# Gated mix of attention and MLP (decode step): the query matrix first in the queue, in eight transfers of 16 partitions

## The chip, the core and the metric

The kernel runs on one core of one Trainium2 chip. The metric is the device time of one launch in microseconds; the time before is the median of three runs. Times inside an execution are counted from the start of the profile's span.

## The reference

For a batch of 8 rows `x` of width 576 (one token each), two branches are computed and mixed by a gate:

```python
g = sigmoid((x * gate_w).sum(-1))
q = x @ wq                            # 576 x 4096: 32 heads of 128
k, v = last 2048 keys of 8192         # 16 kv heads, two query heads share one
a = softmax(q k^T * 128**-0.5) v @ wo # 4096 x 576
b = gelu(layernorm(x) @ w1 + b1) @ w2 + b2   # 576 -> 4608 -> 576
out = g * a + (1 - g) * b
```

All inputs are bf16. What has to be read is mostly the cache: 8 x 16 heads x 2048 keys x 128, for K and for V, 134 MB; the four weight matrices are another 20 MB.

## The kernel before

**Placing and order.** All SBUF data lie in one tensor, `arena`, cut by hand into named regions. Every piece of work is entered in a plan (`_Plan.add`, `_Plan.dma`) with its dependencies; the plan gives each engine its order, and `emit` writes the instructions with semaphore waits. `after=` fixes an order without a wait.

**The load stream.** All large loads go through SyncE's DMA queue (SP), one behind the other, in this order: the small rest of `wq` (rows 512 to 575, 512 KB, L412), the big part of `wq` (rows 0 to 511, 4096 KB, L413), the big part of `w1` (4608 KB, L415), its rest (576 KB, L416), then 32 items of 4096 KB (K and V for 16 units of work, L618), then `w2` (L866) and `wo` (L836). The items go round four slots of 4 MB in the region `RAW`; `wq` lies in slot 0 to begin with and `w1` in slot 3, so that the first items in these slots wait until TensorE has used the matrices (`slot_free = [[o_qp], [], [], [o_hp], ...]`). The first two items, K0 and K1, have free slots and wait for nothing.

**The big part of `wq`.** Partition p of the 128 gets four rows of the matrix, 4p to 4p+3, which are 32 KB in one piece. One transfer carries all 128 partitions (L413). Every other large transfer, too, writes all 128 partitions; K, V and `wq` in rows of 32 KB, `w1` in rows of 36 KB.

**The small inputs.** `x` (8 x 576, partitions 0 to 7, L407), `gate_w` (one row on partition 0, L408), `b1` (four rows on partitions 0 to 3, L409) and `b2` (one row, L856) are issued from ScalarE (ACT), in its own queue, as its first four instructions.

**What the first loads feed.** `x` goes to VectorE (a copy, L421; sums for the layernorm, L433 on) and is transposed by TensorE (L452); `gate_w` is spread over 8 partitions by TensorE (L427) and gives the gate. TensorE's order at the start is: transposes of `x`, the gate's product, the transposes of the normalised `x`, the gate's spreading (L465, L466), then the query product `o_qp` (L501, which waits for both parts of `wq`), then the first product of the MLP, `o_hp` (which waits for `w1` and `b1`), then the bias of the second one (which waits for `b2`). After that the units follow: VectorE transposes K (L718, waits for the K item), TensorE computes the scores (L732), VectorE takes the maximum (L645), ScalarE the exponentials (L649), TensorE multiplies with V (L755 and L188).

**The end.** The products with `w2` and `wo` (L579) follow the last unit; two halves of the output are copied by VectorE and ScalarE (L901, L902) and written by one DMA from SP and one from ACT (L904).

Of the kernel before, what the change touches and what calls it, by code (L numbers as in the profile page):

```python
# [38 lines left out]
class _Plan:  # L39
# [10 lines left out]
    def add(self, eng, fn, deps=(), name=None, cost=0.1, after=(), prio=0):  # L50
        op = _Op(eng, fn, deps, name, cost, after=after, prio=prio)
        op.idx = len(self.all)
        self.all.append(op)
        return op

    def dma(self, eng, fn, semkey, nbytes, deps=(), name=None, after=(), prio=0):
        op = _Op(eng, fn, deps, name, self.DMA_ISSUE, after=after, is_dma=True, dma_sem=semkey, nbytes=nbytes, prio=prio)
        op.idx = len(self.all)
        self.all.append(op)
        return op  # L60
# [106 lines left out]
def _pst(t):  # L167
    return t.ap().ap[0][0]
# [26 lines left out]
def build_kernel(nc, A_x, A_k_cache, A_v_cache, A_wq, A_wo, B_x, B_w1, B_b1, B_w2, B_b2, gate_w, out):  # L195
    B, Sq, D = A_x.shape
    _, Hkv, Sk, Dh = A_k_cache.shape
    Hq = A_wq.shape[1] // Dh
    F = B_w1.shape[1]
# [12 lines left out]
    FC, FT = 4, 36  # L212
# [9 lines left out]
    x2 = A_x.rearrange("b s d -> (b s) d")  # L222
    out2 = out.rearrange("b s d -> (b s) d")

    with ExitStack() as es:
# [70 lines left out]
        arena = es.enter_context(nc.sbuf_tensor("arena", [128, (aoff[0] + 1) // 2], BF))  # L296
        AST = _pst(arena)
        arena_f = arena.bitcast(F32)

        def aoffs(name):  # L300
            return R[name][0] // 2
# [4 lines left out]
        def view(name, parts=128):  # L306
            o, n, dt = R[name]
            a = arena[0:parts, o // 2: o // 2 + (n * (2 if dt == BF else 4)) // 2]
            if dt == F32:
                a = a.bitcast(F32)  # L310
            return a
# [18 lines left out]
        b2_sb = view("b2", 1)  # L330
# [3 lines left out]
        ob = view("ob", 1)  # L334
# [10 lines left out]
        RAW = view("RAW")  # L345
        x_sb, gw_sb, y_bf = view("x_sb", 8), view("gw_sb", 1), view("y_bf", 8)
# [3 lines left out]
        b1c = view("b1c", FC)  # L350
# [4 lines left out]
        wq_m = RAW[:, 0:4 * 4096].rearrange("p (t c) -> p t c", t=4)  # L355
        W1O = (ND - 1) * DE
        WQR = W1O + 4 * F + F // 2
        wq_r = RAW[:, WQR:WQR + 2048]
        w1_m = RAW[:, W1O:W1O + 4 * F].rearrange("p (t c) -> p t c", t=4)
# [20 lines left out]
        add, dma = P.add, P.dma  # L380
# [23 lines left out]
        o_on8 = add("pool", lambda e: e.memset(ones8, 1.0), name="ones8", cost=0.15)  # L404


        d_x = dma("act", lambda e: e.dma_start(x_sb, x2), "x", 8 * D * 2, name="d_x")  # L407
        d_gw = dma("act", lambda e: e.dma_start(gw_sb, gate_w.partition_broadcast(1)), "g", D * 2, name="d_gw", after=[d_x])  # L408
        d_b1 = dma("act", lambda e: e.dma_start(b1c, B_b1.rearrange("(c f) -> c f", c=FC)), "b", F * 2, name="d_b1", after=[d_gw])  # L409
        dx = [d_x]  # L410
        db = [d_b1]
        d_wqr = dma("sp", lambda e: e.dma_start(wq_r, A_wq[512:576, :].rearrange("k (s c) -> (k s) c", s=2)), "wq", 64 * 8192, name="d_wqr")  # L412
        d_wqm = dma("sp", lambda e: e.dma_start(wq_m.rearrange("p t c -> p (t c)"), A_wq[0:512, :].rearrange("(p t) c -> p (t c)", t=4)), "wq", 512 * 8192, name="d_wqm", after=[d_wqr])  # L413
        dwq = [d_wqm, d_wqr]
        d_w1m = dma("sp", lambda e: e.dma_start(w1_m.rearrange("p t c -> p (t c)"), B_w1[0:512, :].rearrange("(p t) c -> p (t c)", t=4)), "w1", 512 * F * 2, name="d_w1m", after=[d_wqm])  # L415
        d_w1r = dma("sp", lambda e: e.dma_start(w1_r, B_w1[512:576, :].rearrange("k (s c) -> (k s) c", s=2)), "w1", 64 * F * 2, name="d_w1r", after=[d_w1m])  # L416
        dw1 = [d_w1m, d_w1r]

# [52 lines left out]
        o_obh = add("act", lambda e: e.activation(out=ob[:, 0:8], in_=ps[0:1, BK_X, 412:420], func=ACTF.Copy), deps=[o_gp, o_homg], name="ob_hi", cost=0.12)  # L471
        o_ob32 = add("act", lambda e: e.activation(out=ot32, in_=ob[:, 0:8], func=ACTF.Copy), deps=[o_obh], name="ob_32", cost=0.12)
        o_obl = add("dve", lambda e: e.tensor_tensor(out=ob[:, 8:16], in0=ps[0:1, BK_X, 412:420], in1=ot32, op=ALU.subtract), deps=[o_ob32], name="ob_lo", cost=0.12)
# [77 lines left out]
        o_hp = add("pe", h_fn, deps=dw1 + db + [o_yT, o_xT, o_gcol, o_homg, o_sel4, o_obl], name="h_pe", cost=5.0)  # L551
# [292 lines left out]
        o_m2, o_bias = [], []  # L844
# [8 lines left out]
            o_m2.append(add("pe", fn, deps=[exp_done[NU - 1], o_mrow, o_mcol], name=name, cost=0.21 * n, after=after))  # L853

        def bias(i):
            d = dma("act", lambda e: e.dma_start(b2_sb, B_b2.partition_broadcast(1)), "b2", D * 2, name="d_b2", after=[d_b1])  # L856
            o_bias.append(AccGroup("m2_b", [(ob[:, 0:8], b2_sb), (ob[:, 8:16], b2_sb)], [d, o_obl, o_obh], cost=0.6, after=[o_hp]).op)

        def m2_chunk(ci):
            s = take_slot()  # L860
# [14 lines left out]

        query(0)
        bias(0)
        for kind, i in stream:
            {"K": k_item, "V": v_item, "W": wo_chunk, "M": m2_chunk, "B": bias}[kind](i)
# [34 lines left out]
def bass_gated_mix__sliding_block_cached__mixer_channel_mlp__decode_kernel(  # L914
    nc: bass.Bass,
    A_x: bass.AP,
    A_k_cache: bass.AP,
    A_v_cache: bass.AP,
    A_wq: bass.AP,
    A_wo: bass.AP,  # L920
    B_x: bass.AP,
    B_w1: bass.AP,
    B_b1: bass.AP,
    B_w2: bass.AP,
    B_b2: bass.AP,
    gate_w: bass.AP,
    out: bass.AP,
):
    build_kernel(nc, A_x, A_k_cache, A_v_cache, A_wq, A_wo, B_x, B_w1, B_b1, B_w2, B_b2, gate_w, out)
# [28 lines left out]
```

## Time and profile before

| | us |
|---|---|
| median of 3 runs | 365.01 (364.51 to 365.36) |
| profiled execution, its own time | 364.83 |
| its span, first to last instruction | 363.3 |
| outside the span | 1.5 |
| VectorE busy | 235.6 |
| TensorE busy (modelled ends) | 299.2 |
| DMA: moved, mean rate over the span | 154.45 MB, 425 GB/s |

The profile's DMA rows give the mean busy share of the core's 16 DMA engines and what they moved. `SPq` and `ACTq` mark the issue of a DMA by that engine's sequencer. In the list of DMA issues the last number is the time from issue to landing. In the table of stages each row has the stretch, its length, the busy time and number of instructions of each engine, the clock granted to TensorE, the DMA share (packets are booked where they start, so that it can pass 1) and the rate.

### The profile page before, as it was taken

The page shows a single profiled execution, that of the slowest core. Times are in us where ns is not written, and L with a number is a line of the kernel's source. Part 1 is how long each engine was busy: PE and PEld are TensorE (multiplying, and loading weights), DVE is VectorE, ACT ScalarE, POOL GpSimd, SP SyncE. Part 2 cuts the span into 40 slices and gives each one's busy share as a digit, 9 for nine tenths or more (in the row PEclk, how much of TensorE's full clock was granted, in tenths as well). Part 3 has the DMA queues.
Part 4 walks back from the last instruction along what each step waited for, and adds up shares of the span by engine and source line. Part 5 has one row for each costly group of instructions (what it writes and reads, how often), then busy time and mean ns, then how long its engine had stood idle before and what let it go on. Part 6 is the DMA issues. An engine that isn't in the chain of part 4 may idle for free.

```text
span 363.3 us, 4819 instructions
## 1 busy us (share of the span) xinstructions
PE 299.2 (82%) x1954; PEld 125.4 (35%) x1423; DVE 235.6 (65%) x166; ACT 168.6 (46%) x130; POOL 22.9 (6%) x52
## 2 busy tenths in 40 slices
PE   1456367999999979998897979898989698999875
PEld 0100000434252615342433417150606152436742
DVE  5522979576776694929385758565675949294720
ACT  1112106656657463664637363838374654655000
POOL 9230030000010000000100000000000000003000
PEclk9976586999999998999999989999999999999999
DMA  8999999999999999999999999999999999999995
GB/s 349 433 429 413 447 419 451 415 451 415 447 415 447 419 448 417 444 422 451 415 455 411 453 411 458 408 458 406 458 411 455 415 449 415 447 419 443 413 430 245
DMA packets 6118, 154.45 MB, mean 425 GB/s; under 512 B 702, under 2 KB 856, under 8 KB 1244
## 3 DMA queue, kind: packets, MB, share of 16 engines
q1 hardware_dynamic: 6064, 154.28, 98.6%
q8 instruction: 8, 0.13, 0.1%
q10 hardware_dynamic: 44, 0.03, 0.1%
q14 instruction: 2, 0.02, 0.0%
HBM read 154.29 MB, written 0.01 MB: 425 GB/s over the span
## 4 chain that ended last, share of the span: by engine, by line
DMA 62%; DVE 24%; PE 12%; SPq 1%; issue 0%
DMA arena<-in_A_k_cache_dram 56%; DVE arena L718 21%; DMA arena<-in_B_w_dram 6%; PE ps L175 5%; DVE arena L668 2%; PE ps L188 2%; PE ps L755 2%; PE ps L732 2%; DVE arena L645 1%; PE ps L579 0%; SPq L415 0%; SPq L416 0%; DVE arena L901 0%; SPq L413 0%; SPq L412 0%
## 5 line engine op out<-in xcount | busy, mean ns | idle before, releaser
L718 DVE STREAM_TRANSPOSE arena<-arena 128x4096 f32<-128x4096 f32 (+1 forms) x34 | 141.7, 4175 | 21.4 <-DMA arena<-in_A_k_cache_dram 21.2
L674 ACT ACTIVATE arena<-arena 32x2048 bf16<-32x2048 bf16 x60 | 114.5, 1908 | 71.2 <-DVE arena L668 42.6
L175 PE MATMUL ps<-arena 128*128 128x512 bf16 (+3 forms) x531 | 137.2, 406 | 0.0
L188 PE MATMUL ps<-arena 128*128 x840 | 109.5, 277 | 7.0 <-issue 0.7
L188 PEld LDWEIGHTS ps<-arena 128*128 x840 | 81.3, 97 | 34.0 <-issue 19.0
L732 PE MATMUL ps<-arena 128*128 128x512 bf16 x128 | 51.2, 400 | 27.4 <-DVE arena L718 25.4
L645 DVE TENSOR_REDUCE arena<-ps 128x1 f32<-128x2048 f32 x16 | 36.7, 2292 | 55.4 <-PE ps L175 55.4
L732 PEld LDWEIGHTS ps<-arena 128*128 128x128 bf16 x128 | 12.6, 98 | 133.1 <-issue 77.0
L649 ACT ACTIVATE arena<-ps,arena 128x2048 bf16<-128x2048 f32 x16 | 40.6, 2540 | 0.5
L646 ACT ACTIVATE arena<-arena 128x1 f32<-128x1 f32 x16 | 3.2, 203 | 64.2 <-DVE arena L645 64.2
L755 PE MATMUL ps<-arena 128*128 128x256 bf16 x184 | 25.3, 273 | 1.2 <-DVE arena L663 1.1
L755 PEld LDWEIGHTS ps<-arena 128*128 128x128 bf16 x184 | 16.9, 99 | 19.3 <-issue 15.0
L668 DVE STREAM_TRANSPOSE arena<-arena 128x1024 f32<-128x1024 f32 x15 | 18.1, 1206 | 2.9 <-ACT arena L649 2.9
L579 PE MATMUL ps<-arena 128*8 128x288 bf16 (+1 forms) x140 | 9.9, 290 | 4.2 <-DMA arena<-in_A_wo_dram 3.2
L739 POOL MEMSET arena<- 128x4096 f32 x1 | 3.5, 3511 | 148.2 <-PE ps L175 148.2
L685 PE MATMUL ps<-arena 128*128 128x512 bf16 x16 | 6.5, 406 | 6.5 <-ACT arena L649 5.2
L629 POOL COPY arena<-arena 32x64 bf16<-32x64 bf16 x16 | 3.7, 229 | 128.2 <-PE ps L175 122.7
L452 PE MATMUL ps<-arena 8*128 8x8 bf16 x8 | 0.6, 171 | 12.8 <-DVE arena L433 7.0
L902 ACT ACTIVATE arena<-ps 8x288 bf16<-8x288 f32 x1 | 0.4, 401 | 19.7 <-PE ps L579 19.7
L579 PEld LDWEIGHTS ps<-arena 128*8 128x8 bf16 (+1 forms) x140 | 5.8, 86 | 10.3 <-issue 3.4
L557 DVE TENSOR_TENSOR arena<-arena 128x1152 f32<-128x1152 f32 x1 | 1.4, 1359 | 11.6 <-ACT arena L555 11.6
L901 DVE CAST arena<-ps 8x288 bf16<-8x288 f32 x1 | 0.4, 446 | 12.3 <-PE ps L579 12.3
(106 smaller groups left out, 101.5 us busy)
## 6 DMA issues: line engine op xcount, KB each, us to landing
arena<-in_A_k_cache_dram SPq DMA_DIRECT2D x16, 4096.0 KB, 28.7
arena<-in_A_v_cache_dram SPq DMA_DIRECT2D x16, 4096.0 KB, 25.5
arena<-in_B_w_dram SPq DMA_DIRECT2D x1, 4608.0 KB, 23.4
arena<-in_A_wo_dram SPq DMA_DIRECT2D x2, 2304.0 KB, 24.0
arena<-in_A_wq_dram SPq DMA_DIRECT2D x1, 4096.0 KB, 13.0
arena<-in_B_w_dram SPq DMA_DIRECT2D x1, 3456.0 KB, 24.4
arena<-in_B_w_dram SPq DMA_DIRECT2D x1, 1152.0 KB, 22.5
arena<-in_B_w_dram SPq DMA_DIRECT2D x1, 576.0 KB, 23.4
```

The costliest lines, as they stand in the source:

```text
L175: return e.add_instruction(mybir.InstMatmult(name=nc.get_next_instruction_name(), engine=mybir.EngineType.PE, ins=[e.lower_ap(rhs), e.lowe ...
L188: return e.add_instruction(mybir.InstMatmult(name=nc.get_next_instruction_name(), engine=mybir.EngineType.PE, ins=[rhs, lhsT], outs=[e.low ...
L579: ins = e.matmul(ps[32 * j:32 * j + 8, BK_ACC, 0:JN], lhsT, rhs[:, JN * j:JN * j + JN], start=False, stop=True, skip_group_check=True, til ...
L629: return e.tensor_copy(dst, src)
L645: mx = add("dve", lambda e: e.tensor_reduce(out=k(g, MX + x), in_=scores, axis=AXL.X, op=ALU.max), deps=[qk_unit[t]], name="mx%d" % t, cos ...
L649: ex = add("act", lambda e: e.activation(out=bass.AP(arena, offset=aoffs("P"), ap=[[AST, 128], [64, 32], [1, 2], [2, 32]]), in_=ps[:, 0:4, ...
L668: pc = add("dve", lambda e: e.transpose(view("PC").bitcast(F32), view("P").bitcast(F32)), deps=[ex] + (sp_done[t - 1][0] if t else [o_acc0 ...
L674: return e.activation(out=bass.AP(arena, offset=32 * a * AST + aoffs(home) + 64 * a, ap=[[AST, 32], [256, 32], [1, 64]]), in_=bass.AP(aren ...
L685: mm = e.matmul(*args, start=True, stop=False, skip_group_check=True) if n == 0 else held_matmul(nc, e, *args, start=True, stop=False, ski ...
L718: return e.transpose(bass.AP(arena_f, offset=foffs(base) + 2048 * h0, ap=[[AST // 2, 128], [1, 2048 * nh]]), bass.AP(arena_f, offset=foffs ...
L732: mm = e.matmul(*args, start=False, stop=True, skip_group_check=True) if rc == 0 else held_matmul(nc, e, *args, stop=True, skip=True)
L755: return e.matmul(dst, bass.AP(arena, offset=aoffs(home) + 256 * q + ee, ap=[[AST, 128], [2, 128]]), slot(s).rearrange("p (r k d) -> p r k ...
```

## The change

The big part of `wq` comes first in SP's queue, in eight transfers. Transfer q carries 16 of the 128 partitions: q, q+8, q+16, ..., q+120, a row of 32 KB each, 512 KB in all. Behind the first transfer stands `x`, behind the second `gate_w`, behind the third `b1`, behind the fourth `b2`; then come the other four transfers, the rest of `wq`, and `w1` as before. All are issued from SP; ACT issues none at the start any more. What goes where in SBUF is the same, and so are the bytes. The query product waits for all nine transfers of `wq`.

```diff
-        d_x = dma("act", lambda e: e.dma_start(x_sb, x2), "x", 8 * D * 2, name="d_x")
-        d_gw = dma("act", ..., "g", D * 2, name="d_gw", after=[d_x])
-        d_b1 = dma("act", ..., "b", F * 2, name="d_b1", after=[d_gw])
-        d_wqr = dma("sp", ..., "wq", 64 * 8192, name="d_wqr")
-        d_wqm = dma("sp", lambda e: e.dma_start(wq_m.rearrange("p t c -> p (t c)"), A_wq[0:512, :].rearrange("(p t) c -> p (t c)", t=4)), "wq", 512 * 8192, name="d_wqm", after=[d_wqr])
-        dwq = [d_wqm, d_wqr]
+        first = []
+
+        def early(fn, key, nbytes, name):
+            d = dma("sp", fn, key, nbytes, name=name, after=first[-1:])
+            first.append(d)
+            return d
+
+        def wq_part(q):
+            return early(lambda e: e.dma_start(bass.AP(arena, offset=q * AST + aoffs("RAW"), ap=[[8 * AST, 16], [1, 4 * 4096]]), A_wq[0:512, :].rearrange("(i q t) c -> q i (t c)", q=8, t=4)[q]),
+                         "wq", 64 * 8192, "d_wqm%d" % q)
+        dwq = [wq_part(0)]
+        d_x = early(lambda e: e.dma_start(x_sb, x2), "x", 8 * D * 2, "d_x")
+        dwq.append(wq_part(1))
+        d_gw = early(..., "g", D * 2, "d_gw")
+        dwq.append(wq_part(2))
+        d_b1 = early(..., "b", F * 2, "d_b1")
+        dwq.append(wq_part(3))
+        d_b2 = early(..., "b2", D * 2, "d_b2")
+        dwq += [wq_part(q) for q in range(4, 8)]
+        d_wqr = early(..., "wq", 64 * 8192, "d_wqr")
+        dwq.append(d_wqr)
...
         def bias(i):
-            d = dma("act", lambda e: e.dma_start(b2_sb, B_b2.partition_broadcast(1)), "b2", D * 2, name="d_b2", after=[d_b1])
```

`AST` is the step from one partition of `arena` to the next, so `[8 * AST, 16]` names 16 partitions that stand eight apart.

More of the change, by code (lines that the diff above doesn't have):

```diff
@@ L404, in build_kernel @@
         o_on8 = add("pool", lambda e: e.memset(ones8, 1.0), name="ones8", cost=0.15)
[L407 to L412, printed above, removed]
@@ L413, in build_kernel @@
-        d_wqm = dma("sp", lambda e: e.dma_start(wq_m.rearrange("p t c -> p (t c)"), A_wq[0:512, :].rearrange("(p t) c -> p (t c)", t=4)), "wq", 512 * 8192, name="d_wqm", after=[d_wqr])
-        dwq = [d_wqm, d_wqr]
-        d_w1m = dma("sp", lambda e: e.dma_start(w1_m.rearrange("p t c -> p (t c)"), B_w1[0:512, :].rearrange("(p t) c -> p (t c)", t=4)), "w1", 512 * F * 2, name="d_w1m", after=[d_wqm])
+        first = []
[3 more added lines that the diff above has]
+            return d
@@ new lines, in wq_part @@
+        def wq_part(q):
[4 more added lines that the diff above has]
+        dwq.append(wq_part(1))
+        d_gw = early(lambda e: e.dma_start(gw_sb, gate_w.partition_broadcast(1)), "g", D * 2, "d_gw")
@@ new lines, in build_kernel @@
+        dwq.append(wq_part(2))
+        d_b1 = early(lambda e: e.dma_start(b1c, B_b1.rearrange("(c f) -> c f", c=FC)), "b", F * 2, "d_b1")
+        dwq.append(wq_part(3))
+        d_b2 = early(lambda e: e.dma_start(b2_sb, B_b2.partition_broadcast(1)), "b2", D * 2, "d_b2")
+        dwq += [wq_part(q) for q in range(4, 8)]
+        d_wqr = early(lambda e: e.dma_start(wq_r, A_wq[512:576, :].rearrange("k (s c) -> (k s) c", s=2)), "wq", 64 * 8192, "d_wqr")
+        dwq.append(d_wqr)
+        dx, db = [d_x], [d_b1]
@@ L416, in build_kernel @@
+        d_w1m = dma("sp", lambda e: e.dma_start(w1_m.rearrange("p t c -> p (t c)"), B_w1[0:512, :].rearrange("(p t) c -> p (t c)", t=4)), "w1", 512 * F * 2, name="d_w1m", after=[d_wqr])
         d_w1r = dma("sp", lambda e: e.dma_start(w1_r, B_w1[512:576, :].rearrange("k (s c) -> (k s) c", s=2)), "w1", 64 * F * 2, name="d_w1r", after=[d_w1m])
@@ L855, in bias @@
         def bias(i):
-            d = dma("act", lambda e: e.dma_start(b2_sb, B_b2.partition_broadcast(1)), "b2", D * 2, name="d_b2", after=[d_b1])
-            o_bias.append(AccGroup("m2_b", [(ob[:, 0:8], b2_sb), (ob[:, 8:16], b2_sb)], [d, o_obl, o_obh], cost=0.6, after=[o_hp]).op)
+            o_bias.append(AccGroup("m2_b", [(ob[:, 0:8], b2_sb), (ob[:, 8:16], b2_sb)], [d_b2, o_obl, o_obh], cost=0.6, after=[o_hp]).op)
         def m2_chunk(ci):
```

## The prediction

> **What bounds the kernel now.** I read the page first, its DMA lines above all:
>
> ```profile
> span 363.3 us, 4819 instructions
> ...
> DMA  8999999999999999999999999999999999999995
> ...
> q1 hardware_dynamic: 6064, 154.28, 98.6%
> ```
>
> SP's queue, q1, keeps all 16 DMA engines busy 98.6% of the span; no compute engine comes near that. Next the table of stages, to see whether the rate depends on what is loaded:
>
> ```profile
> 4.50:14.30 9.80, 1.50 (x16) 0.72 (x16) 7.99 (x14) 0.80 (x3) 6.04 (x7) 1.00 1.02 436
> 14.30:26.50 12.20, 7.86 (x56) 2.02 (x30) 3.62 (x9) 1.59 (x6) 4.22 (x19) 0.86 1.00 430
> 45.00:180.00 135.00, 121.11 (x705) 46.66 (x488) 96.31 (x49) 74.00 (x53) 5.34 (x9) 0.95 1.01 434
> 180.00:337.00 157.00, 140.04 (x884) 62.05 (x652) 107.42 (x70) 86.67 (x63) 3.51 (x1) 0.99 1.00 432
> ```
>
> The last number is GB/s. `wq`, `w1` and the cache, three layouts in HBM, all run at 430 to 436. So the ceiling is not in the source but in the engines or in the way into SBUF, and a microsecond added to this stream is a microsecond of time. The chain of waits ends on it:
>
> ```profile
> 337.04 22.52 DMA arena<-in_B_w_dram
> 359.60 1.75 PE ps L579 x24
> ```
>
> The stream's last piece lands at 359.6; what follows (products, copies, output DMA) takes 3.7 us and the change leaves it alone but for one issue. Then the DMA issues, for the price of the piece that is changed:
>
> ```profile
> arena<-in_A_k_cache_dram SPq DMA_DIRECT2D x16, 4096.0 KB, 28.7
> arena<-in_A_wq_dram SPq DMA_DIRECT2D x1, 4096.0 KB, 13.0
> arena<-in_A_wq_dram SPq DMA_DIRECT2D x1, 512.0 KB, 3.7
> ```
>
> A K item is issued 28.7 us before it lands and takes 9.7 to move (4.19 MB at 433 GB/s): nearly two others always stand ahead of it, so the queue doesn't run dry. Last, the first microseconds:
>
> ```profile
> 0.80 0.41 SPq L412 DMA_DIRECT2D arena<-in_A_wq_dram  x1
> 0.81 0.59 ACTq L407 DMA_DIRECT2D arena<-in_A_x_dram  x1
> 1.27 0.41 SPq L413 DMA_DIRECT2D arena<-in_A_wq_dram  x1
> 1.73 1.33 SPq L415 DMA_DIRECT2D arena<-in_B_w_dram  x1
> 3.37 3.48 DVE L421 COPY arena<-arena 8x128 bf16<-8x128 bf16 x1 [3.37 <-DMA arena<-in_A_x_dram]
> 15.21 0.62 PE L501 MATMUL ps<-arena 128*32 128x512 bf16 x4
> 19.70 0.53 SPq L618 DMA_DIRECT2D arena<-in_A_v_cache_dram  x1
> ```
>
> `x` is there at 3.37, the query product starts at 15.21, and V0, which needs `wq`'s slot, is issued at 19.70.
>
> **The big part of `wq`, 16 partitions at a time.** Now the rest of `wq` lands at 0.80+3.7 = 4.5 and the big part at 1.27+13.0 = 14.3: 9.8 us for 4.19 MB, 1.22 for each eighth. No transfer of size in this trace writes fewer than 128 partitions, so the price of an eighth that reaches only 16, eight apart, must be bounded. Lower end: each of the 16 engines still moves one 32 KB row in the same 1.22 us, and the eight cost nothing. Upper end: engines that write neighbouring groups of partitions share a way in and take turns by two, 2.44 us each, 8 x 1.22 = 9.8 us more. The rows say only that the ceiling is common to three sources and that everything that reaches it spreads over all 128 partitions, which is what the change takes away. If the ceiling were the engines', the first end holds; if it is the way in, the second. I take the second: a limit so even from source to source is most simply one at the common destination.
>
> [...]
>
> **The start.** Today the first transfer has 4 KB rows and meets `x` and `gate_w` from the other queue on the same engines; its 16 completions spread from 3.75 to 4.54 (the trace's semaphore events), and the slowest engine sets the end. With one 32 KB row per engine first, up to this 0.8 is won; if the small rows now hold up the queue instead (`x` with 8 rows, the others with one or four), up to 0.3 is lost. I take 0.5 won. Twelve more completions among the transfers: 0.1 at most, taken as 0.1.
>
> **SP's issues.** Thirteen stand ahead of `w1` instead of two. The row nearest in kind, 0.41, and 0.23 to 0.59 for the small ones (their rows on ACT) make about 0.9 for a large and a small one together, less than the 1.22 that an eighth moves at its fastest: hidden. If each large one cost 1.33 as L415 did, the first four pairs would come every 1.9 and the others every 1.33: 4 x 0.7 + 4 x 0.1 = 3.2 us of gaps at the fast rate, none at the slow rate of 2.44. K0 and K1, now issued at 3.6, move to about 9 (18 at the worst), and the queue has `wq` and `w1` ahead of them until 26.5. Hidden.
>
> **The small inputs.** `x` stands behind the first eighth: at 0.80+3.7 = 4.5, or 5.7 if shared, plus 0.1. L421 waits for it; it starts at 3.37 but ends only at 6.85, where its twin at 13.78 takes 0.23, so something else holds it and an `x` at 5.8 is still in time. Without that cover VectorE's chain, with TensorE's transposes behind it, moves by 2.4 at most, from 15.2 to 17.6, while `wq` itself would be 9.5 later, at 23.8. `gate_w` (about 8, used at 7.2), `b1` (10.5, used at 26.5) and `b2` (13, used at 32.5) lie under the same cover. ACT loses four issues (1.4 us) at a time when its next work is at 10.97. The output's ACT issue becomes the first DMA of that queue; the first one took 0.59 where the output's took 0.30. SP's own ends 0.11 later, so 0 to 0.2; I take 0.1.
>
> **What waits for `wq`.** SP waits for the query product before V0, with all later items behind it. That goes from 19.7 to about 29; V0's turn comes when K1 has moved, 47 before and 56 after. 27 us of cover. `o_hp` and K2 move along (32.65 to 42, due at 66). So nothing multiplies the delay and nothing absorbs it: VectorE, the next in line, waits for K at every unit already.
>
> **The sum.** +9.8 -0.5 +0.1 +0.1 = +9.5. The profiled execution took 364.83 (363.3 span and 1.5 around it): 374.3. The median of the runs lies 0.18 above it; I say 374.4.
>
> **The rivals.**
> 1. *The ceiling is the engines'* and 16 rows on 16 engines are as good as 128: -0.5 +0.2 = -0.3, 364.5 to 365. For it: an eighth has one row for each engine, just as the large transfer has eight. Chance 0.13.
> 2. *Faster:* the ceiling is the engines', the start wins the whole 0.8, and the small costs vanish: 364.0. It decides on the engine that ends last, if that one was also late at 4.54 and gets nothing else in its way. Chance 0.05.
> 3. *Taking turns is uneven:* one engine of a pair goes first until it is through four eighths and moves to other partitions, and its partner then runs alone; the loss is half, 4.9: 369.4. Likewise SP's slow issues without sharing: +3.2 -0.3, 367.7. Together 0.10; against the latter, only one of the first four issues was slow.
> 4. *It doesn't do what it says:* `x` is not earlier but later, 4.6 to 5.8 instead of 3.37. That holds in all cases and costs nothing, as above.
>
> **How the numbers follow.** Full sharing has 0.72. Its own range is 373.6 to 375.5 (start between -0.8 and +0.3, ACT's issue 0 to 0.2, a median 0.2 off). Down to 368.5 it also takes in uneven sharing; same, faster and the slow issues, about 0.2, stay out. 0.2% is 0.7 us, about what a measurement of this kernel can tell from no change (the three runs spread by 0.85): slower 0.82, same 0.13, faster 0.05.
>
> **What would show it.** In the stage table the stretch 4 to 20 at about 215 GB/s instead of 433, and the stream at 433 from about 24 on; the query product starting near 24; the first K transposes (37.45) near 47; the tail after the last `w2` landing 3.7 as before. I am wrong if 4 to 14 still shows 430: then the end is within 0.7 of before. Uneven sharing would show 280 to 300 over the first 19 us.

## The result, and the profile after

| | us | ratio to before |
|---|---|---|
| before, median of 6 runs | 364.84 (364.51 to 365.36) | 1 |
| changed, median of 6 runs | 375.27 (375.03 to 377.43) | 1.0294 [1.0272, 1.0315] |
| changed, run again, 4 runs | 375.25 (375.13 to 375.56) | 1.0289 [1.0272, 1.0306] |

The change costs 10.4 us; 9.4 were forecast. The lines below are from a second profiled execution of the changed kernel (375.17, span 373.7), because in the first (377.43) the rows of the transfers on 128 partitions ran 12% slower up to 44.7 us (24.1 instead of 27.0 GB/s per engine).

The table of stages of the changed kernel, columns as before (the last is GB/s), answers the first question, whether the rate falls while the big part of `wq` moves:

```profile
4.00:14.00 10.00, 1.33 (x9) 0.47 (x9) 5.35 (x13) 0.80 (x3) 6.53 (x7) 1.00 1.02 212
14.00:24.00 10.00, 1.23 (x10) 1.12 (x10) 1.45 (x9) 0.38 (x2) 2.36 (x11) 1.00 0.98 226
24.00:38.00 14.00, 7.47 (x50) 1.45 (x28) 2.47 (x2) 1.21 (x4) 1.83 (x8) 0.83 1.03 442
50.00:190.00 140.00, 122.60 (x701) 46.67 (x488) 101.64 (x50) 73.60 (x52) 5.34 (x9) 0.95 1.00 432
```

It does: 212 GB/s where before had 436, and 442 as soon as `w1` follows. The last but one column says more: the 16 engines are as busy at 212 GB/s (1.02) as at 432 (1.00). They are not short of work; each row of 32 KB takes twice as long (2.54 us against 1.21, from the trace's packet records). The page of the profile says the same of the queue, a busy share no lower than before (98.6%):

```profile
span 373.7 us, 4807 instructions
...
q1 hardware_dynamic: 6204, 154.30, 98.7%
```

The timeline of the changed kernel (start, duration, engine, line; in brackets the idle time before and what ended it) shows the steps that follow. L435, L515 and L917 are now the lines of the copy of `x`, the query product and the output's DMAs:

```profile
0.80 0.62 SPq L415 DMA_DIRECT2D arena<-in_A_wq_dram  x1
...
6.05 0.81 DVE L435 COPY arena<-arena 8x128 bf16<-8x128 bf16 x1 [6.05 <-DMA arena<-in_A_x_dram]
...
24.82 0.62 PE L515 MATMUL ps<-arena 128*32 128x512 bf16 x4 [9.20 <-DMA arena<-in_A_wq_dram]
...
372.17 0.58 ACTq L917 DMA_DIRECT2D out_dram<-arena  x1
372.21 0.31 SPq L917 DMA_DIRECT2D out_dram<-arena  x1
```

`x` comes 2.7 us later (3.37 before), but its copy ends at 6.86 as before (6.85). The query product starts at 24.82. Before it started at 15.21, but `wq` had landed at 14.3; so `wq` itself is 10.5 later. The chain of waits, at its end:

```profile
347.54 22.39 DMA arena<-in_B_w_dram
369.98 1.73 PE ps L593 x24
```

The landing that the last group of products waits for first moved from 359.60 to 369.98, by 10.4: what is lost on `wq` goes through the whole stream undiluted. What comes after it takes 3.7 us, as before. The very last row of `w2` ends a little after that landing, at 360.63 before and 371.01 now in the packet records, again 10.4 apart.

### The profile page after: what moved, and what is told of

The parts are those of the page before. It is cut to its first block, busy times and chain, and to the rows that moved or that the text cites. A ratio compares the mean times of both kernels' runs of the same rounds, so it can differ in the third digit from the quotient of the medians.

```text
span 376.0 us, 4807 instructions
## 1 busy us (share of the span) xinstructions
PE 295.3 (79%) x1935; PEld 125.1 (33%) x1423; DVE 232.0 (62%) x166; ACT 168.6 (45%) x130; POOL 22.9 (6%) x52
## 4 chain that ended last, share of the span: by engine, by line
DMA 55%; DVE 21%; PE 20%; SPq 2%; issue 1%
DMA arena<-in_A_k_cache_dram 49%; DVE arena L732 18%; PE ps L175 8%; PE ps L188 6%; DMA arena<-in_B_w_dram 6%; PE ps L746 3%; PE ps L769 2%; DVE arena L682 2%; DVE arena L659 1%; SPq L415 1%; PE ps L593 0%; PE ps L699 0%; SPq L426 0%; SPq L418 0%; SPq L422 0%
## 5 line engine op out<-in xcount | busy, mean ns | idle before, releaser
L175 PE MATMUL ps<-arena 128*128 128x512 bf16 (+3 forms) x524 | 134.8, 398 | 13.8 <-DVE arena L732 10.9
L746 PE MATMUL ps<-arena 128*128 128x512 bf16 x122 | 48.6, 398 | 19.6 <-DVE arena L732 17.7
L515 PE MATMUL ps<-arena 128*32 128x512 bf16 (+1 forms) x40 | 5.6, 552 | 9.8 <-DMA arena<-in_A_wq_dram 9.8
L530 DVE CAST arena<-ps 128x1024 bf16<-128x1024 f32 x1 | 1.2, 1224 | 12.6 <-PE ps L175 12.6
## 6 DMA issues: line engine op xcount, KB each, us to landing
arena<-in_B_w_dram SPq DMA_DIRECT2D x1, 3456.0 KB, 24.1
```

The costliest lines, as they stand in the source:

```text
L175: return e.add_instruction(mybir.InstMatmult(name=nc.get_next_instruction_name(), engine=mybir.EngineType.PE, ins=[e.lower_ap(rhs), e.lowe ...
L515: ins = e.matmul(out_of(c, i), lhs(t, c), rhs_of(t, c, i), start=first, stop=last, skip_group_check=True, tile_position=(0, 32 * c))
L746: mm = e.matmul(*args, start=False, stop=True, skip_group_check=True) if rc == 0 else held_matmul(nc, e, *args, stop=True, skip=True)
```

## The experiments

The traces' packet records give the length of single rows. Where one time is given for the rows of a kernel, it is the median of these records.

### Is it the small transfers or the few partitions? `e1_columns`, `e2_split_only`, `e3_neighbours`, `e4_source`

The first kernel keeps the eight transfers of 512 KB, their order and the small inputs, but lets each reach all 128 partitions, with a row of 4 KB:

```diff
-            return early(lambda e: e.dma_start(bass.AP(arena, offset=q * AST + aoffs("RAW"), ap=[[8 * AST, 16], [1, 4 * 4096]]), A_wq[0:512, :].rearrange("(i q t) c -> q i (t c)", q=8, t=4)[q]),
+            return early(lambda e: e.dma_start(RAW[:, 2048 * q:2048 * q + 2048], A_wq[0:512, :].rearrange("(p t) c -> p (t c)", t=4)[:, 2048 * q:2048 * q + 2048]),
```

> Eight transfers of 512 KB with the small inputs between them as in the changed kernel, but each transfer carries an eighth of the columns to all 128 partitions (rows of 4 KB) instead of all columns to 16 partitions. Theory A, the destination (16 partitions eight apart reach SBUF by half as many ways as 128): the loss goes away, 365.0 to 366.0; the 4 KB rows themselves cost 8 x 8 x 7 ns = 0.5 us (the 4 KB rows of the rest of wq took 159 ns each, an eighth of a 32 KB row 152). The stretch from 4 to 14 us shows 410 to 430 GB/s. Theory C, many small transfers and their completions: stays at 374 to 376. Theory D, small inputs in the big queue: stays at 374 to 376. Theory B, the source (rows 256 KB apart are read together): it goes away here too.

Measured 366.58 (365.92 to 366.79), ratio 1.0045 [1.0028, 1.0062]: 1.7 us over before, where the change has 10.4. Its first stage:

```profile
4.00:14.00 10.00, 1.27 (x9) 0.48 (x9) 8.02 (x14) 0.80 (x3) 6.54 (x7) 1.00 1.01 378
```

So neither the number of transfers nor their size nor the order makes the bulk of the loss. The 1.7 are more than expected, and the rate, 378 instead of 410 or more, shows where they arise: in the first 10 us some of the 4 KB rows ran at 3 to 9 GB/s per engine, where most had 25.8 (packet records). What the 96 rows below 20 GB/s took beyond the usual 0.16 us comes to 1.3 us per engine. Why they were slow is not settled.

The second is the kernel before with one edit, the big part of `wq` in the eight strided transfers; the small rest of `wq` stays first and the small inputs stay on ACT:

```diff
-        d_wqm = dma("sp", lambda e: e.dma_start(wq_m.rearrange("p t c -> p (t c)"), A_wq[0:512, :].rearrange("(p t) c -> p (t c)", t=4)), "wq", 512 * 8192, name="d_wqm", after=[d_wqr])
+        for q in range(8):
+            dwq.append(dma("sp", lambda e, q=q: e.dma_start(bass.AP(arena, offset=q * AST + aoffs("RAW"), ap=[[8 * AST, 16], [1, 4 * 4096]]), A_wq[0:512, :].rearrange("(i q t) c -> q i (t c)", q=8, t=4)[q]),
+                           "wq", 64 * 8192, name="d_wqm%d" % q, after=dwq[-1:]))
```

> The kernel before with one part of the change alone: the big part of wq in eight transfers of 16 partitions eight apart; the rest of wq stays first in the queue, the small inputs stay on ACT. Theories A, B and C: 374.5 to 375.5, the whole loss. Theory D, the small inputs between the transfers: 365.

Measured 375.89 (375.75 to 376.6), 1.0308 [1.0291, 1.0325]: 11.0 us over before, 0.4 above the top of what was expected. The split alone carries the whole loss, without the small inputs in SP's queue (theory D). Why it costs 0.6 more than the change is not settled; in its records some rows of `w1`, which here follow the split transfers directly, take up to 2.69 us instead of 1.36.

The third takes 16 neighbouring partitions for each transfer instead of 16 that stand eight apart:

```diff
-            ... bass.AP(arena, offset=q * AST + aoffs("RAW"), ap=[[8 * AST, 16], [1, 4 * 4096]]), A_wq[0:512, :].rearrange("(i q t) c -> q i (t c)", q=8, t=4)[q]),
+            ... RAW[16 * q:16 * q + 16, 0:4 * 4096], A_wq[0:512, :].rearrange("(p t) c -> p (t c)", t=4)[16 * q:16 * q + 16, :]),
```

> The changed kernel with other sixteens: transfer q carries partitions 16q to 16q+15, neighbours, and the rows of the matrix that belong to them. If sharing goes by neighbouring partitions in fours, four engines share a way in: each 32 KB row takes twice the 2.55 us of the changed kernel, 8 x 5.1 = 41 us for the big part against 20.4, so about 395 (theory A). If every transfer of 16 partitions costs the same whatever partitions it names (C, or a limit by count): 375. Theory B, source rows 256 KB apart: here they are 32 KB apart as in the kernel before, so 365.

Measured 391.21 (390.74 to 391.54), 1.0722 [1.0704, 1.0739]. Its stages and the query product:

```profile
4.00:14.00 10.00, 1.33 (x9) 0.47 (x9) 2.79 (x5) 0.00 (x0) 5.97 (x6) 1.00 0.94 106
...
24.00:38.00 14.00, 0.00 (x0) 0.00 (x0) 0.00 (x0) 0.00 (x0) 0.00 (x0) 1.00 0.92 104
```

```profile
41.03 0.62 PE L515 MATMUL ps<-arena 128*32 128x512 bf16 x4 [21.50 <-DMA arena<-in_A_wq_dram]
```

Nothing differs from the change but which 16 partitions a transfer reaches (and with them which rows of the source, which the fourth kernel takes up), and the rate halves once more, with the engines again busy (0.94). A row takes 4.57 us against 1.21 on 128 partitions, 3.8 times as long. The whole was expected 4 us slower still; the row had been put at 5.1.

The fourth keeps the 16 partitions eight apart in SBUF, but reads 16 neighbouring rows of the source (the rows of the query matrix then lie in exchanged places, so that the queries are other ones):

```diff
-A_wq[0:512, :].rearrange("(i q t) c -> q i (t c)", q=8, t=4)[q]),
+A_wq[0:512, :].rearrange("(p t) c -> p (t c)", t=4)[16 * q:16 * q + 16, :]),
```

> The changed kernel with the source alone changed: transfer q reads the rows of the matrix that lie together in HBM (512 KB in one piece), and writes them to the same partitions eight apart as in the changed kernel; the rows of the matrix so stand on other partitions, and the queries are made from a matrix with its rows exchanged. Theory A, the destination: nothing changes, 375.0 to 375.6. Theory B, the source: back to 365. If both count, in between.

Measured 374.92 (374.82 to 375.45), 1.0275 [1.0258, 1.0292], within 0.4 us of the change and 0.1 below what was expected. Its first stage has the rate of the change:

```profile
4.00:14.00 10.00, 1.33 (x9) 0.47 (x9) 5.45 (x13) 0.80 (x3) 6.54 (x7) 1.00 1.00 212
```

A source in one piece wins nothing: the destination decides, as the third kernel says from the other side.

### Which partitions share a way? `e5_four_apart`, `e6_32_four_apart`, `after_again`, `e7_small_on_sp`

A way is here the author's estimate of what lies behind the rates: what engines share where their writes to a set of partitions are slowed together. The runs show rates and row times, not the ways themselves. `after_again` is the changed kernel itself, for the profile shown above. In `e5_four_apart` a transfer takes 16 partitions four apart within one half of SBUF; in `e6_32_four_apart` four transfers take 32 partitions four apart over all of it:

```diff
-            ... offset=q * AST + aoffs("RAW"), ap=[[8 * AST, 16], [1, 4 * 4096]]), ...("(i q t) c -> q i (t c)", q=8, t=4)[q]),
+            ... offset=(64 * (q // 4) + q % 4) * AST + aoffs("RAW"), ap=[[4 * AST, 16], [1, 4 * 4096]]), ...("(h i r t) c -> h r i (t c)", h=2, r=4, t=4)[q // 4, q % 4]),
```

```diff
-            ... offset=q * AST + aoffs("RAW"), ap=[[8 * AST, 16], [1, 4 * 4096]]), ...("(i q t) c -> q i (t c)", q=8, t=4)[q]),
+            ... offset=q * AST + aoffs("RAW"), ap=[[4 * AST, 32], [1, 4 * 4096]]), ...("(i q t) c -> q i (t c)", q=4, t=4)[q]),
```

> The changed kernel with other sixteens: transfers 0 to 3 carry partitions q, q+4, ..., q+60 and transfers 4 to 7 the same in the upper half, with the rows of the matrix that belong to them. Every sixteen names each group of four neighbours in one half once, so nothing is shared inside a group of four; what is left is sharing between groups. If groups 32 partitions apart share a way in: two engines each, as in the changed kernel, 374.5 to 375.6. If it is groups 64 apart: none share here, 365 to 366. If only neighbours shared, also 365 to 366 (but then the changed kernel, eight apart, would have lost nothing either). [...]

> The changed kernel with four transfers of 32 partitions four apart (q, q+4, ..., q+124; 1 MB each) instead of eight of 16 eight apart. All groups of four are named, so every way in is in use; each engine has two rows. If the rows are dealt to the engines so that each engine stays with its own way in, nothing is shared: 365 to 366. If they are dealt by count, two consecutive rows to an engine, all first rows are eight apart, as in the changed kernel, and two share again: 374.5 to 375.6. If one row with the next in the same half at once, in between.

> The changed kernel itself, on the chip of the other runs of this call, for a profile beside them. Its first profile had every 32 and 36 KB row up to 44.7 us 12% longer than later ones, also on 128 partitions, and was 2.1 us over its other runs. If that was a disturbance of one execution: 375.0 to 375.5, and the rows of w1 at 1.364 us as in the kernel before. If it belongs to the kernel: w1 at 1.53 again.

`e5_four_apart`: 375.36 (375.11 to 375.43), 1.0287 [1.0271, 1.0304], as slow as the change. `e6_32_four_apart`: 365.20 (364.95 to 365.39, 10 runs), 1.0011 [1.0002, 1.002]. `after_again`: 375.25, with the rows of `w1` at 1.364 us as in the kernel before. The first stage of `e5_four_apart` and of `e6_32_four_apart`, in this order:

```profile
4.00:14.00 10.00, 1.33 (x9) 0.47 (x9) 5.13 (x13) 0.80 (x3) 6.56 (x7) 1.00 1.02 212
```

```profile
4.00:14.00 10.00, 1.33 (x9) 0.47 (x9) 5.55 (x14) 0.80 (x3) 6.54 (x7) 1.00 1.05 447
```

In `e5_four_apart` the 16 partitions fill one half, 0 to 63 or 64 to 127, with steps of four, and still run at half rate (212 GB/s). Take four neighbours as one group, an estimate from the quarter rate of `e3_neighbours` (106 GB/s): then a group would share its way with another group of the same half. Groups 64 apart do not explain it, because no sixteen here has two of them. Which groups of a half share was not shown: the first case of the expectation gives the rates of all these kernels, but so would groups 16 apart. In `e6_32_four_apart` the rows have their 1.22 us and the full rate (447 GB/s), with the same strided form and the same small inputs between. So it is neither the stride nor the splitting, but the set of partitions that one transfer writes; counted in ways, an estimate from 447, 212 and 106 GB/s, all of them in 32 partitions four apart, half of them in the change, a quarter in `e3_neighbours`. A limit by the number of partitions alone falls with `e3_neighbours`, which has 16 like the change and half its rate; sets of 32 partitions other than four apart were not run.

The last of the four takes the other half of the change by itself: `wq` in two transfers as before, the small rest first, but `x`, `gate_w` and the biases on SP between the two:

```diff
+        d_wqr = early(..., "wq", 64 * 8192, "d_wqr")
         d_x = early(lambda e: e.dma_start(x_sb, x2), "x", 8 * D * 2, "d_x")
         d_gw = early(..., "g", D * 2, "d_gw")
         d_b1 = early(..., "b", F * 2, "d_b1")
         d_b2 = early(..., "b2", D * 2, "d_b2")
+        d_wqm = early(..., "wq", 512 * 8192, "d_wqm")
```

> The other part of the change alone: the small inputs move to SP's queue, behind the rest of wq (first, as before) and ahead of the big part, which goes whole to 128 partitions as before. Theory D, the small inputs hold up the big queue: 366 or more. Theory A: no loss from them; 364.3 to 365.3, where the output's DMA on ACT, now the first of its queue (0.58 us to issue in the changed kernel, 0.30 in the kernel before), may cost 0.2, and an undisturbed start may win 0.3.

Measured 365.73 (365.19 to 366.03, 12 runs), 1.002 [1.001, 1.003]: 0.9 us, between the two ranges that were expected. The big transfer is now issued at 2.52 instead of 1.27, behind five others. In the records its first row starts 0.2 later than before (3.57 against 3.40), but its last row ends 1.4 later (15.24 against 13.86). With the small inputs between large transfers there is no such price: `e6_32_four_apart` took 365.20, and the same four transfers with the small inputs on ACT took 365.15 (`e9_32_act`, below). So the 0.9 are more likely a price of this order than of SP's queue; where in the queue they arise was not taken further.

### Is there a gain in the order, and what are the 0.4 of 32 rows? `e8_big_first`, `e9_32_act`

`e8_big_first` is the kernel before with only the order of the two parts of `wq` exchanged. `e9_32_act` has the four transfers of `e6_32_four_apart` first, the small rest behind them, and the small inputs on ACT as before:

```diff
-        d_wqr = dma("sp", ..., name="d_wqr")
-        d_wqm = dma("sp", ..., name="d_wqm", after=[d_wqr])
+        d_wqm = dma("sp", ..., name="d_wqm")
+        d_wqr = dma("sp", ..., name="d_wqr", after=[d_wqm])
```

```diff
-        d_wqm = dma("sp", ..., name="d_wqm", after=[d_wqr])
+        for q in range(4):
+            dwq.append(dma("sp", lambda e, q=q: e.dma_start(bass.AP(arena, offset=q * AST + aoffs("RAW"), ap=[[4 * AST, 32], [1, 4 * 4096]]), A_wq[0:512, :].rearrange("(i q t) c -> q i (t c)", q=4, t=4)[q]),
+                           "wq", 128 * 8192, name="d_wqm%d" % q, after=dwq[-1:]))
```

> The kernel before with the order alone changed: the big part of wq first, whole and to 128 partitions, the rest of wq behind it; the small inputs stay on ACT. If the forecast's gain at the start exists (one 32 KB row for each engine first instead of 4 KB rows, up to 0.8 us): 364.0 to 364.5. If the start is set by something else: 364.7 to 365.0.

> The big part first in four transfers of 32 partitions four apart, as in the run that lost 0.4, but with the small inputs on ACT as in the kernel before. What is left of the 0.4 then belongs to the split and the order; what goes belongs to the small inputs in SP's queue and to the output's issue on ACT as the first of its queue (0.58 us instead of 0.30). Expected: half of it goes, 364.8 to 365.0; if the small inputs cost nothing, 365.2.

`e8_big_first`: 364.92 (364.8 to 365.3, 12 runs), 1.0002 [0.9991, 1.0013]. The half microsecond that the forecast took off for large rows at the start does not exist: the last packet of `wq` ends at 14.0 us in the records, 13.9 in before.

`e9_32_act`: 365.15 (364.92 to 365.25, 12 runs), 1.0008 [0.9999, 1.0017]. Half of the 0.4 of `e6_32_four_apart` was expected to go with the small inputs back on ACT, and it did not go. The traces put it elsewhere. First issues of before, whose first transfer reaches 128 partitions, stand in the prediction with 0.41 us; here is the first issue of `e6_32_four_apart`:

```profile
0.80 0.56 SPq L415 DMA_DIRECT2D arena<-in_A_wq_dram  x1
```

The records have the first packet at 2.15 in both kernels with 32 rows (2.19 in the change), at 1.85 in before and 1.84 in `e8_big_first`. This 0.3 stays to the end; the last landing in the chains of waits of `e6_32_four_apart`, `e9_32_act` and `e8_big_first`, 359.60 in before:

```profile
359.88 1.73 PE ps L592 x24
```

```profile
359.95 1.74 PE ps L582 x24
```

```profile
359.62 1.71 PE ps L579 x24
```

The first issue of `e3_neighbours`, with 16 partitions too, but neighbours, is short, and its first packet stands at 1.82:

```profile
0.80 0.39 SPq L415 DMA_DIRECT2D arena<-in_A_wq_dram  x1
```

So the late start goes with the strided set, or with the hand-built address pattern in which all strided sets here are written, and not with the small number of partitions. It is read from these traces; no run was made for it. No version beats the kernel before; `e8_big_first` equals it.

## Why the prediction was right, step by step

- **The big part of `wq`** (+9.8): right in kind, too small in size. Two engines taking turns was the upper end, an assumption that no row of before shows, and the run went beyond it: a row takes 2.48 us in the mean (2.54 in the median) instead of 2.44, and from the first packet of the big part to the end of its last it is 20.7 us (2.19 to 22.91 in the records), where before has 10.5 (3.40 to 13.86). That is +10.2, not +9.8. The rows of the kernel before could not decide between the engines and the way in; the prediction chose by an argument. The choice, a limit at the common destination and not at the engines, is what `e3_neighbours` (391.21 with other partitions) and `e4_source` (374.92 with other rows of the source) bear out.
- **The start** (−0.5): wrong. Nothing is won (`e8_big_first`), and the first strided transfer starts 0.3 later. From −0.5 to about +0.2, with the small rest of `wq` 0.1 shorter at its new place, this is the term that was most off.
- **Completions** (+0.1) **and the output's ACT issue** (+0.1): the issue is indeed 0.58 instead of 0.30, but from the landing at 369.98 to the end it is 3.7 as before: the last packet is still one of SP's, 2.2 us after the last one of `w2` in both. Nothing for either is left over: 10.2 + 0.2 = 10.4, the whole difference of that landing. The forecast 9.5 lay 0.9 below, made up of 0.4 at the rows, 0.7 at the start and −0.2 here.
- **The total**: 364.83 + 9.5 + 0.18 is 374.5; the prediction wrote 374.4. The measured 375.27 lies 0.2 below the top of the range given for full sharing (373.6 to 375.5). The two largest errors had the same sign, and it took only these 0.2 more to leave that range: the mechanism was right, that the time stayed inside is in part luck.
- **SP's issues**: hidden, as said. They take 0.43 to 0.62 each; the thirteen ahead of `w1` are through by 8.2, and `w1` is needed in the queue at 23.
- **The small inputs**: `x` was forecast for 4.6 to 5.8 and said to be in time then. It came at 6.05, a little later, and was in time all the same: the copy ends at the same moment. Rival 4 happened, as the text said it would in all cases, and cost nothing.
- **What waits for `wq`**: V0 is issued at 29.3 (about 29 forecast), with K1 still ahead of it, and K2 at 43.2 (42). The delay goes through undiluted: the query product at 24.82 (near 24), the first transposes of K at 48.0 (near 47), each late by what the rows and the start were short. One reading was wrong: VectorE does not wait for K at every unit. Before it waited for K ten times (21.2 us in all), in the changed kernel eleven times (21.6). The delay goes through because the stream itself ends later.
- **The rivals**: if the engines had been the ceiling, 4 to 14 us would have shown 430; it shows 212. Uneven sharing would have shown 280 to 300 and 369; from transfer to transfer the mean row stays at 2.2 to 2.6 us. Slow issues without sharing (367.7) fall with the busy share of 1.02: the engines did not wait for work in that stretch.

## What to carry to other kernels

When a load stream is the bound, as it is here (SP's queue busy 98.6% of the span), ask of every piece of a cut transfer which partitions it writes. In this kernel, with 436 GB/s before, 16 partitions eight apart ran at 212, 16 neighbours at 106, 32 partitions four apart at 447, and all 128 with an eighth of the columns at 378 in the first 10 us. The cut itself won nothing here: by columns it cost 1.7 us, by 32 partitions 0.4. A DMA share of 1 did not mean that the engines were used well: it was 1.02 at 212 GB/s and 1.00 at 432. Read the GB/s beside it, stage by stage, and compare it with a stage whose transfers write all 128 partitions. And do not price a start by the spread of its completions: here the 0.8 us of spread were no time to be won (`e8_big_first`).

## What the runs showed of the hardware that was not expected

- The median row of 32 KB ran at 27.0 GB/s per engine in a transfer on 128 partitions (1.21 us), at 12.9 in the change (2.54) and at 7.16 in `e3_neighbours` (4.57). Two engines of the change together have 25.8, less than one at 27.0; four of `e3_neighbours` have 28.6.
- 32 rows on 32 partitions four apart ran at 27.0 GB/s per engine (`e6_32_four_apart`). The expectation left open how rows are dealt to the engines; that was not shown.
- Four transfers of 1 MB behind one another cost no more than one of 4 MB, apart from the later first packet (0.3 us of the 0.4 in `e9_32_act`: 365.15 against 364.72 for the kernel before, beside it).
- Rows of 4 KB in transfers whose rows stand 32 KB apart in the source reached 378 GB/s in their first 10 us, against 447 for the 32 KB rows of `e6_32_four_apart` in the same stretch.
- The first DMA that ACT issued took 0.59 us to issue at the start of the program (before) and 0.58 at its end (the changed kernel); ACT's issue at the end took 0.30 where others had gone ahead of it.
